# Two key matmuls of the first tile between the opening transposes, and tile 2's copies ahead of the first feature map

## The chip, the cores and the metric

The kernel runs on one core of a Trainium2 chip. The time is the device time of one execution in microseconds (us). A core has a matrix engine (TensorE, "PE" in the profile; its weight loads are "PEld"), a vector engine (VectorE, "DVE"), a scalar engine (ScalarE, "ACT"), GpSimd ("POOL") and SyncE ("SP"), which here only issues transfers. Each engine works through its own queue in order and waits on semaphores of the others. Matmul results land in PSUM, in eight banks of 128 x 512 f32; VectorE and ScalarE read them from there.

## The reference, cut to what matters

```python
qkv = x @ wqkv                       # x: 2048 x 512, 32 heads of 16
phi = lambda t: where(t > 0, t + 1, exp(t)) + 1e-6
pq, pk = phi(q), phi(k)
kv = einsum("bhsd,bhse->bhde", pk, v);  z = einsum("bhsd->bhd", pk)
a  = (pq @ kv) / (pq . z + 1e-6) @ wo          # linear attention
h  = layernorm(x)                              # over the 512 features
b  = (gelu(h^T @ w1 + b1) @ w2 + b2)^T         # MLP over the 2048 tokens
g  = sigmoid((x * gate_w).sum(-1))
out = g * a + (1 - g) * b
```

## The kernel before

The 2048 tokens are 16 tiles of 128 (`NT`), the 512 features 4 blocks of 128 (`ND`). The kernel uses `kv = pk^T v = (x^T pk)^T wv`, so that it needs the keys first and no values: for each tile it makes the keys (`kacc`, four matmuls), their feature map (`pk`), and then adds `x^T pk` to four banks `gacc` (`g_tile`, four matmuls). This key stage takes the first 33 us. After it come the queries (`qacc`) between the first MLP matmuls (`uacc`), the rest of the first MLP layer, and the output loop with `aps` and `yps`.

The schedule is written out by hand (`manual_schedule`): each engine runs its instructions in the order in which the code lists them. Semaphores and the choice of PSUM banks follow from the buffers named; all banks come from one pool of eight (`bank`).

The key matmuls need x with features on the partitions (`xT`). For tiles 3 to 15 a transposing transfer makes it (L135). For tiles 0 to 2 PE transposes: four 128 x 128 matmuls with the identity into a bank `pt`, of which VectorE copies the first half to `xT` (L209) and ScalarE the second (L210). The order around the change is this (L287 to L295):

```python
transpose_tile(0)
transpose_tile(1)
for t in range(2):
    k_part(t, range(2))
transpose_tile(2)
ln_step(0)
for t in range(HEADS):
    k_part(t, range(2 if t < 2 else 0, ND))
    k_phi(t)
```

So PE does the transposes of tiles 0 and 1, the first two of the four key matmuls of tile 0 and of tile 1, the transposes of tile 2, and then the rest. `k_phi` is an exponential on ScalarE (L214), a minimum with one on VectorE (L215) and a combination on VectorE that writes `pk` (L218). `ln_step(u)` is the layernorm statistics of tile u on VectorE (L238, L239), and for each fourth tile a short step towards the inverse deviation (L243 and, on POOL, L244). In the loop that follows, tile t's keys are made, `g_tile` runs four tiles behind (`LAG`) and the statistics three tiles behind (`LN_LAG`); at the end of the stage four `g_tile` calls remain, the last of which needs `pk` of tile 15.

The transfers of the opening: SP's queue brings x tiles 0, 1 and 2 one by one, ScalarE's queue the key weights in two halves. Six matmuls on constants (`wps`) come first on PE.

Of the kernel before, what the change touches and what calls it, by code (L numbers as in the profile page):

```python
# [7 lines left out]
ACT = mybir.ActivationFunctionType  # L8
# [7 lines left out]
def kernel(  # L16
# [13 lines left out]
    nc = tc.nc  # L30
    P = nc.NUM_PARTITIONS
# [9 lines left out]
    ND = D // P  # L41
# [25 lines left out]
    def keep(shape, dtype, name):  # L67
        return persist.tile(shape, dtype, name=name, tag=name)

    def bank(name, dtype=FP32):  # L70
        return ps.tile([P, SC], dtype, name=name, tag="bank")

    xs = keep([P, NT, D], BF16, "xs")
    hs = keep([P, NT, D], BF16, "hs")
    xT = keep([P, ND, S], BF16, "xT")
# [17 lines left out]
    ident = keep([P, P], BF16, "ident")  # L93
# [18 lines left out]
    def mm(o, lhsT, rhs, start, stop, **kw):  # L112
        nc.tensor.matmul(o, lhsT=lhsT, rhs=rhs, start=start, stop=stop, **kw)  # L113
# [20 lines left out]
    def load_xT(t0, n):  # L134
# [14 lines left out]
        out=ident[:], in_=ident[:], compare_op=ALU.not_equal, fill=1.0, base=0,  # L149
# [5 lines left out]
        out=maskQ[:], in_=maskH[:].rearrange("p (a m) -> p m a", m=2), op=ALU.max, axis=AX.X  # L155
# [4 lines left out]
        out=xT[:, :, 3 * P : 3 * P + 2],  # L160
        in_=xs[:, 0, 0 : 2 * ND].rearrange("p (k c) -> p k c", k=ND),
# [10 lines left out]
    for c, (j0, nb) in enumerate(w1_chunks):  # L172
        w = wpool.tile([P, NT, FB * P], BF16, name="w1c", tag="wc")
        w1c.append(w)
        for t0 in range(0, NT, 8) if c < 3 else (0,):
            t1 = t0 + 8 if c < 3 else NT
            nc.sync.dma_start(
                out=w[:, t0:t1, : nb * P], in_=w1_view[:, t0:t1, j0 * P : (j0 + nb) * P]
# [15 lines left out]
    def warm_up(n, cols=SC):  # L194
        for _ in range(n):
            mm(wps[:, :cols], warm[:, 0:P], warm[:, :cols], True, True)
# [2 lines left out]
    nc.scalar.activation(out=act_warm[:], in_=ones_f[:], func=ACT.Exp)  # L199
    warm_up(6)  # L200

    def transpose_tile(t):
        pt = bank("pt")
        for k in range(ND):
            mm(pt[:, k * P : (k + 1) * P], xs[:, t, k * P : (k + 1) * P], ident[:], True, True)
        H = ND // 2
        src = pt[:].rearrange("p (k s) -> p k s", k=ND)
        dst = xT[:, :, t * P : (t + 1) * P]
        nc.vector.tensor_copy(out=dst[:, 0:H], in_=src[:, 0:H])  # L209
        nc.scalar.activation(out=dst[:, H:], in_=src[:, H:], func=ACT.Copy)  # L210

    def phi(dst, acc):
        e = work.tile([P, SC], BF16, name="e", tag="e", bufs=6)
        nc.scalar.activation(out=e[:], in_=acc[:], func=ACT.Exp)  # L214
        nc.vector.tensor_scalar(  # L215
            out=e[:], in0=e[:], scalar1=1.0, scalar2=PHI_EPS, op0=ALU.min, op1=ALU.add
        )
        nc.vector.scalar_tensor_tensor(  # L218
            out=dst, in0=acc[:], scalar=0.0, in1=e[:], op0=ALU.max, op1=ALU.add
        )  # L220
# [3 lines left out]
    def k_part(t, ks):  # L224
        if t not in kaccs:
            kaccs[t] = bank("kacc")
        for k in ks:
            mm(
                kaccs[t][:], xT[:, k, t * P : (t + 1) * P], wk_sb[:, k, :],
                k == 0, k == ND - 1,  # L230
            )

    def k_phi(t):
        phi(pk[:, t, :], kaccs.pop(t))

    def ln_stats(t):
        stats = work.tile([P, nc.vector.BN_STATS_DIM], FP32, name="stats", tag="stats", bufs=2)
        nc.vector.bn_stats(out=stats[:], in_=xs[:, t, :])  # L238
        nc.vector.bn_aggr(out=mv[:, t, :], in_=stats[:])  # L239

    def ln_rstd(g):
        s = slice(g * TPC, (g + 1) * TPC)
        nc.vector.tensor_scalar_add(out=veps[:, s], in0=mv[:, s, 1], scalar1=EPS)  # L243
        nc.gpsimd.tensor_tensor(out=rstd[:, s], in0=veps[:, s], in1=mhalf[:], op=ALU.pow)  # L244
# [36 lines left out]
    def ln_step(u):  # L281
        ln_stats(u)
        if u % TPC == TPC - 1:
            ln_rstd(u // TPC)

    HEADS = 3
    transpose_tile(0)  # L287
    transpose_tile(1)
    for t in range(2):
        k_part(t, range(2))  # L290
    transpose_tile(2)
    ln_step(0)
    for t in range(HEADS):
        k_part(t, range(2 if t < 2 else 0, ND))
        k_phi(t)  # L295
    ln_step(1)
# [159 lines left out]
    for j in range(NB0, NF):  # L456
# [19 lines left out]
        out=gg[:], in0=gth[:], scalar1=0.5, scalar2=0.5, op0=ALU.mult, op1=ALU.add  # L476
    )
    nc.vector.tensor_scalar(
        out=c1[:], in0=gth[:], scalar1=-0.5, scalar2=0.5, op0=ALU.mult, op1=ALU.add
# [3 lines left out]
    for t in range(NT):  # L483
        c, tl = divmod(t, TPC)
        aps = bank("aps")
        for j in range(ND):
# [3 lines left out]
            out=a_sc[:], in_=aps[:], func=ACT.Identity,  # L490
            scale=gg[:, t : t + 1], bias=c2[:, t : t + 1],
        )
        for c0, W in ((0, D - P), (D - P, P)) if t == NT - 1 else ((0, D),):
            cs = slice(c0, c0 + W)
            yps = bank("yps")
            for f in range(NF):
# [6 lines left out]
                out=ot[:, :W], in0=yps[:, :W], scalar=c1[:, t : t + 1], in1=a_sc[:, cs],  # L503
# [35 lines left out]
```

## Time and profile before

| | |
|---|---|
| median of five runs | 164.31 us (164.02 to 164.57) |
| profiled execution, its own time | 164.49 us |
| its span | 162.80 us |
| PE busy | 158.8 us, 98% of the span |
| VectorE busy | 89.9 us, 55% |
| ScalarE busy | 63.1 us, 39% |
| key stage ends (first `uacc` matmul starts) | 33.42 us |

The span runs from the first to the last recorded instruction of the profiled execution; its own time is 1.69 us longer. Starts are counted from the span's start. A matmul of 128 x 512 is shown with a length of 0.38 us, but the next starts before it ends; the distance of starts is what counts. In rows of groups the last part tells how long the engine was idle just before and what ended that.

### The profile page before, as it was taken

To read this page: it belongs to the slowest core of one execution; us is meant where nothing else is said; L and a number is where in the kernel's file an instruction comes from. 1 tells how busy PE (TensorE), PEld (TensorE's weight loads), DVE (VectorE), ACT (ScalarE), POOL (GpSimd) and SP (SyncE) were. 2 spreads that over 40 slices of the span, in tenths; PEclk is the share of its full clock that TensorE was granted. 3 is DMA by queue.
4 is the path that set the end of the run, shared out by engine and by line. 5 is a ranking of instruction groups with operands and counts; after the bars stand their busy time and mean duration, and the time that the engine had idled before them with its cause. 6 is when DMAs were issued, how large, how long until landed. Compare 5 with 4: busy or idle time off the path is not lost.

```text
span 162.8 us, 2191 instructions
## 1 busy us (share of the span) xinstructions
PE 158.8 (98%) x833; PEld 72.6 (45%) x833; DVE 89.9 (55%) x212; ACT 63.1 (39%) x98; POOL 17.4 (11%) x34
## 2 busy tenths in 40 slices
PE   7999999999999999999999999999999999999993
PEld 2444444444444444444444444444444444444452
DVE  1599999967999999509995401256211111111112
ACT  3453284848667473212865113111122222111110
POOL 3000702200010000001515500050000000000000
PEclk9999999999999999999999999999999999999999
DMA  5999999999900006600891699832000001110001
GB/s 168 235 259 215 296 348 322 382 386 385 296 7 0 0 0 214 237 4 0 274 331 61 218 317 316 294 115 83 32 32 32 32 32 38 47 46 33 32 32 32
DMA packets 30569, 25.18 MB, mean 155 GB/s; under 512 B 8480, under 2 KB 29984, under 8 KB 30560
## 3 DMA queue, kind: packets, MB, share of 16 engines
q1 hardware_dynamic: 28288, 21.89, 43.2%
q0 software_dynamic: 1440, 2.38, 5.3%
q10 hardware_dynamic: 832, 0.79, 1.4%
q8 instruction: 6, 0.10, 0.2%
q14 instruction: 3, 0.02, 0.0%
HBM read 21.11 MB, written 2.23 MB: 143 GB/s over the span
## 4 chain that ended last, share of the span: by engine, by line
PE 96%; DMA 2%; SPq 0%; DVE 0%; issue 0%
PE uacc L113 30%; PE yps L113 30%; PE kacc L113 9%; PE gacc L113 9%; PE qacc L113 8%; PE aps L113 8%; DMA xs<-in_A_x_dram 2%; PE denps L113 1%; PE pt L113 1%; PE kvps L113 0%; SPq L129 0%; PE w2ps L113 0%; DVE ot L502 0%; PE pt L332 0%
## 5 line engine op out<-in xcount | busy, mean ns | idle before, releaser
L113 PE MATMUL uacc<-hs,w1c 128*128 128x512 bf16 x224 | 51.3, 379 | 0.0
L113 PE MATMUL yps<-uT,w2c 128*128 128x512 bf16 (+2 forms) x238 | 51.0, 366 | 0.0
L502 DVE SCALAR_TENSOR_TENSOR ot<-yps,c,a_sc 128x512 bf16<-128x512 f32 (+2 forms) x17 | 12.2, 720 | 44.9 <-PE yps L113 44.8
L113 PEld LDWEIGHTS <-w2c 128*128 128x128 bf16 x238 | 22.8, 98 | 25.9
L113 PEld LDWEIGHTS <-w1c 128*128 128x128 bf16 x224 | 21.8, 98 | 26.3 <-issue 0.2
L489 ACT ACTIVATE a_sc<-aps,c,gg 128x512 f32<-128x512 f32 x16 | 12.4, 777 | 46.7 <-PE aps L113 39.9
L326 ACT ACTIVATE uT<-uacc,bcol 128x512 bf16<-128x512 f32 x14 | 9.3, 687 | 21.7 <-PE uacc L113 21.7
L113 PE MATMUL kacc<-wk_sb,xT 128*128 128x512 bf16 x64 | 16.7, 392 | 0.0
L113 PE MATMUL qacc<-xT,wq_sb 128*128 128x512 bf16 x64 | 16.4, 379 | 0.0
L113 PE MATMUL aps<-W2sb,pqT 128*128 128x512 bf16 x64 | 16.4, 379 | 0.0
L113 PE MATMUL gacc<-pk,xs 128*128 128x512 bf16 x64 | 15.9, 379 | 0.0
L254 ACT ACTIVATE hs<-xs,nmr,rstd 128x512 bf16<-128x512 bf16 x16 | 12.8, 806 | 3.1 <-DVE nmr L248 3.1
L214 ACT ACTIVATE e<-qacc 128x512 bf16<-128x512 f32 x16 | 9.6, 597 | 9.2 <-PE qacc L113 9.2
L441 POOL DMA_DIRECT2D rex<-rd_dram x16 | 9.4, 598 | 22.5 <-DVE pqT L443 20.3
L214 ACT ACTIVATE e<-kacc 128x512 bf16<-128x512 f32 x16 | 9.3, 592 | 6.6 <-DVE mv L239 2.3
L113 PEld LDWEIGHTS <-xs 128*128 128x128 bf16 x76 | 7.4, 102 | 9.3 <-DMA xs<-in_A_x_dram 1.2
L218 DVE SCALAR_TENSOR_TENSOR pk<-kacc,e 128x512 bf16<-128x512 f32 x16 | 11.1, 692 | 0.6
L218 DVE SCALAR_TENSOR_TENSOR pqT<-qacc,e 128x512 bf16<-128x512 f32 x16 | 11.1, 692 | 0.6
L238 DVE BATCH_NORM_STATS2 stats<-xs 128x6 f32<-128x512 bf16 x16 | 10.9, 683 | 0.0
L215 DVE TENSOR_SCALAR e<-e 128x512 bf16<-128x512 bf16 x32 | 9.0, 281 | 2.3 <-ACT e L214 2.1
L428 DVE CUSTOM_DVE_ANT_0 junk<-xs,gw_b 128x512 bf16<-128x512 bf16 x16 | 9.8, 685 | 0.0
L279 DVE TENSOR_TENSOR zacc<-zacc,pk 128x512 f32<-128x512 f32 x14 | 9.6, 685 | 0.2
(61 smaller groups left out, 70.6 us busy)
## 6 DMA issues: line engine op xcount, KB each, us to landing
w1c<-in_B_w_dram SPq DMA_DIRECT2D x7, 1024.0 KB, 10.7
w2c<-in_B_w_dram SPq DMA_DIRECT2D x8, 896.0 KB, 6.0
rex<-rd_dram POOLq DMA_DIRECT2D x16, 128.0 KB, 3.8
out_dram<-ot SPq DMA_DIRECT2D x13, 128.0 KB, 1.7
xs<-in_A_x_dram SPq DMA_DIRECT2D x3, 512.0 KB, 4.1
wk_sb<-in_A_wqkv_dram ACTq DMA_DIRECT2D x2, 256.0 KB, 3.4
xs<-in_A_x_dram SPq DMA_DIRECT2D x4, 128.0 KB, 2.7
wq_sb<-in_A_wqkv_dram SPq DMA_DIRECT2D x1, 512.0 KB, 6.2
```

What stands on the lines that cost most here:

```text
L113: nc.tensor.matmul(o, lhsT=lhsT, rhs=rhs, start=start, stop=stop, **kw)
L214: nc.scalar.activation(out=e[:], in_=acc[:], func=ACT.Exp)
L215: nc.vector.tensor_scalar(out=e[:], in0=e[:], scalar1=1.0, scalar2=PHI_EPS, op0=ALU.min, op1=ALU.add)
L218: nc.vector.scalar_tensor_tensor(out=dst, in0=acc[:], scalar=0.0, in1=e[:], op0=ALU.max, op1=ALU.add)
L238: nc.vector.bn_stats(out=stats[:], in_=xs[:, t, :])
L254: nc.scalar.activation(out=hs[:, t, :], in_=xs[:, t, :], func=ACT.Identity, scale=rstd[:, t : t + 1], bias=nmr[:, t : t + 1],)
L279: nc.vector.tensor_tensor(out=zacc[:], in0=first, in1=pk[:, t, :], op=ALU.add)
L326: nc.scalar.activation(out=uT[:, j, :], in_=acc[:], func=ACT.Gelu_apprx_tanh, bias=bcol[:, j : j + 1])
L428: nc.vector.tensor_tensor_reduce(out=junk[:], in0=xs[:, t, :], in1=gw_b[:], scale=1.0, scalar=0.0, op0=ALU.mult, op1=ALU.add, accum_out=gp ...
L441: nc.gpsimd.dma_start(out=rex[:], in_=src.unsqueeze(1).to_broadcast([8, HEAD, SC]))
L489: nc.scalar.activation(out=a_sc[:], in_=aps[:], func=ACT.Identity, scale=gg[:, t : t + 1], bias=c2[:, t : t + 1],)
L502: nc.vector.scalar_tensor_tensor(out=ot[:, :W], in0=yps[:, :W], scalar=c1[:, t : t + 1], in1=a_sc[:, cs], op0=ALU.mult, op1=ALU.add,)
```

## The change

Transposing is done in parts, each with a `pt` bank of its own and one copy, on VectorE or on ScalarE. Tile 0 is split in three: block 0 (VectorE), block 1 (VectorE), blocks 2 and 3 (ScalarE). Tiles 1 and 2 are split in two halves. The first two key matmuls of tile 0 now stand right after tile 0's transposes, ahead of those of tile 1. The rest of tile 0's key matmuls and its feature map stand after tile 2's transposes and ahead of tile 0's statistics (`ln_step(0)`), which stood before all feature maps.

```diff
+    def transpose_part(t, k0, k1, on_act):
+        pt = bank("pt")
+        for k in range(k0, k1):
+            mm(pt[:, k * P : (k + 1) * P], xs[:, t, k * P : (k + 1) * P], ident[:], True, True)
+        src = pt[:, k0 * P : k1 * P].rearrange("p (k s) -> p k s", k=k1 - k0)
+        dst = xT[:, k0:k1, t * P : (t + 1) * P]
+        if on_act:
+            nc.scalar.activation(out=dst, in_=src, func=ACT.Copy)
+        else:
+            nc.vector.tensor_copy(out=dst, in_=src)
+
     def transpose_tile(t):
-        pt = bank("pt")
-        for k in range(ND):
-            mm(pt[:, k * P : (k + 1) * P], xs[:, t, k * P : (k + 1) * P], ident[:], True, True)
-        H = ND // 2
-        src = pt[:].rearrange("p (k s) -> p k s", k=ND)
-        dst = xT[:, :, t * P : (t + 1) * P]
-        nc.vector.tensor_copy(out=dst[:, 0:H], in_=src[:, 0:H])
-        nc.scalar.activation(out=dst[:, H:], in_=src[:, H:], func=ACT.Copy)
+        transpose_part(t, 0, ND // 2, False)
+        transpose_part(t, ND // 2, ND, True)
...
     HEADS = 3
-    transpose_tile(0)
+    transpose_part(0, 0, 1, False)
+    transpose_part(0, 1, 2, False)
+    transpose_part(0, 2, ND, True)
+    k_part(0, range(2))
     transpose_tile(1)
-    for t in range(2):
-        k_part(t, range(2))
+    k_part(1, range(2))
     transpose_tile(2)
+    k_part(0, range(2, ND))
+    k_phi(0)
     ln_step(0)
-    for t in range(HEADS):
+    for t in range(1, HEADS):
         k_part(t, range(2 if t < 2 else 0, ND))
         k_phi(t)
     ln_step(1)
```

## The prediction

> **What bounds the kernel now.** I read the page first, then the chain of waits stage by stage, then the timelines of TensorE (PE) and VectorE (DVE) for the first 34 us. The page's parts 1 and 4:
>
> ```profile
> PE 158.8 (98%) x833; PEld 72.6 (45%) x833; DVE 89.9 (55%) x212; ACT 63.1 (39%) x98; POOL 17.4 (11%) x34
> ...
> PE 96%; DMA 2%; SPq 0%; DVE 0%; issue 0%
> ```
>
> PE is the bound over the whole span, so whatever lengthens PE's queue moves the end one for one: after 36 us no view names a wait of PE longer than 0.4 us. The edit lies in the first 10 us; so the question is which engine ends each wait there. PE's timeline:
>
> ```profile
> 3.36 0.63 PE L113 MATMUL pt<-ident,xs 128*128 128x128 bf16 x4
> 4.25 0.61 PE L113 MATMUL pt<-ident,xs 128*128 128x128 bf16 x4 [0.27 <-DMA xs<-in_A_x_dram]
> 4.66 1.75 PE L113 MATMUL kacc<-wk_sb,xT 128*128 128x512 bf16 x4
> 6.24 0.39 PE L113 MATMUL pt<-ident,xs 128*128 128x128 bf16 x4
> 6.46 3.62 PE L113 MATMUL kacc<-wk_sb,xT 128*128 128x512 bf16 x16
> ```
>
> Columns: start, length, work. Call the transposes of tiles 0, 1, 2 T0, T1, T2 and a tile's key matmuls K0, K1 and so on. From 4.25 PE runs T1, two matmuls each of K0 and K1, T2, the rest, with no hole. The one hole is between T0's last start plus a pitch (3.36 + 4 x 0.107 = 3.79) and tile 1's landing, 4.25. Four key matmuls from 4.66 take 1.58 us up to T2, with starts 0.42 apart; from 6.46 sixteen take 3.46, 0.216 apart. So the array doubles its pace near 6.1.
>
> VectorE's timeline, same columns:
>
> ```profile
> 6.67 0.42 DVE L209 CAST xT<-pt 128x256 bf16<-128x256 f32 x1 [1.34 <-PE pt L113]
> 7.01 0.68 DVE L238 BATCH_NORM_STATS2 stats<-xs 128x6 f32<-128x512 bf16 x1
> 7.72 0.18 DVE L239 BATCH_NORM_AGGREGATE mv<-stats 128x2 f32<-128x6 f32 x1
> 8.03 0.29 DVE L215 TENSOR_SCALAR e<-e 128x512 bf16<-128x512 bf16 x1
> 8.36 0.69 DVE L218 SCALAR_TENSOR_TENSOR pk<-kacc,e 128x512 bf16<-128x512 f32 x1
> ...
> 10.81 0.68 DVE L238 BATCH_NORM_STATS2 stats<-xs 128x6 f32<-128x512 bf16 x1
> 11.53 0.18 DVE L239 BATCH_NORM_AGGREGATE mv<-stats 128x2 f32<-128x6 f32 x1
> 11.63 0.26 DVE L215 TENSOR_SCALAR e<-e 128x512 bf16<-128x512 bf16 x1
> ...
> 31.82 0.69 DVE L218 SCALAR_TENSOR_TENSOR pk<-kacc,e 128x512 bf16<-128x512 f32 x1
> ```
>
> From 8.03 on VectorE shows no idle entry up to the last pk at 31.82: a rigid chain of phi and statistics. Only tile 0's statistics are free: they fill the time in which VectorE would wait for tile 0's exponential. And this chain touches PE once, in the chain of waits:
>
> ```profile
> 29.07 3.45 PE gacc L113 x16
> 32.53 0.03 issue
> 32.56 1.02 PE gacc L113 x4
> ```
>
> The last four gacc matmuls (G15) need pk of tile 15. It ends at 31.82 + 0.69 = 32.51; G15 starts at 32.56. At full pitch it would have started at 32.15 + 0.216 = 32.37, so PE already waits 0.19 us for VectorE. **VectorE's chain, not PE, sets when the key stage ends**, with PE 0.19 behind it.
>
> **What the Trainium skill says.** "TensorE: Matmul & The Clock Gate", What's actually happening: the array runs at half rate until a free-running window of about 3.4 us has been busy. The trace agrees on the two rates (0.427 and 0.216 us a matmul, change near 6.1) and shows no window. "VectorE: DVE Perf Modes", Why PSUM operands drop a tier: an f32 PSUM source goes at one element a cycle; 0.424 us for 256 elements and 0.680 for 512 (gT) give 1.0 ns an element, which agrees. "PSUM — Partial Sum Buffer", PSUM bank collisions raise a hardware error: two engines' accesses to one bank must be ordered, reads too. The waits agree, here one tile's two copies:
>
> ```profile
> ACT xT L210 <- DVE xT L209: 3.0, 3, 1.4
> ```
>
> ScalarE's copy starts only after VectorE's, three times.
>
> **The change part by part.**
>
> *Copies in banks of their own.* T0 gets three banks, T1 and T2 two each. ScalarE's halves no longer follow VectorE's: T0's could start about 0.4 us earlier, T2's too. Tile 0's copy on VectorE becomes two of 128 elements. Not in the trace: 0.424 - 128 x 1.0 = 0.296 us each by the two sizes above (bounds 0.21, a pure half, and 0.42, nothing saved). One instruction more on VectorE, in a stretch where it is idle. No instruction on ACT, POOL or SP moves and no DMA is added, moved or passed.
>
> *K0's first two matmuls before T1.* T0's first part ends at 3.36 + 0.31 = 3.67; its copy runs 3.71 to 4.01 (a wait costs 0.04 in the rows: 3.99 to 4.03), the second to 4.30. With 0.06 to the weight load and 0.10 for it, K0 starts at 4.17 and 4.60. T1 then runs 5.02 to 5.45 in place of 4.25. The hole is hardly filled: 4.17 against 4.25, a gain of 0.08.
>
> *A new stall.* K1 now follows T1 directly and must wait for T1's VectorE copy, which K0's two matmuls used to cover. T1's first half ends at 5.13 + 0.31 = 5.44, the copy at 5.48 + 0.42 = 5.90, K1 starts at 6.06: PE is idle for 6.06 - 5.45 = 0.61. Bounds: 0.5 if load and wait overlap, 0.7 if not. Everything in PE's queue stands behind it: K1, T2, K0's rest. With the pace doubling near 6.12 as before, K1's second is at 6.30 and T2 at 6.52, against 6.24: **PE +0.28**. Tile 2 lands at 1.73 + 4.1 = 5.83 (issue plus its time to landing), so T2 could in no order start before about 5.9.
>
> *T2's copies ahead of the first feature map; statistics of tile 0 after it.* In the program's order VectorE now has T2's copy, phi of tile 0, statistics of tile 0, phi of tile 1. The exponential of tile 0 was held by T2's ACT copy (7.12 to 7.40); now K0's end holds it: its last matmul starts at 6.52 + 4 x 0.056 + 0.216 = 6.96 and ends 0.38 later, 7.34. Exponential 7.39 to 7.99, VectorE's first phi step at 8.02, against 8.03: **-0.01**. The ACT copy (6.95 to 7.33) is off the path; if it took 0.1 us more it would be on it. The statistics leave the free slot and enter the rigid chain: from 10.81 to the next phi step at 11.63 a pair costs **0.82**. The slot they leave, 7.25 to 8.02, stays empty. Below: 0.4 if the first phi could start as soon as tile 2's landing allows (near 7.65); above: 1.1 if the stall is at its upper bound and the clock a little later.
>
> *Banks further on.* By the order of the buffers K5 still waits for pk of tile 1. It ends at 9.97 now and at 10.78 then; K5 starts at 10.78 + 0.28 = 11.06. Cost nothing, with 0.28 of cover left; without it, PE would lose the lack, still inside the slack at G15. K6 to K15 wait for pk four tiles back: K6's slack was 12.51 - 10.90 = 1.6 us, and later ones have more.
>
> *Sum.* pk of tile 15 ends at 32.51 - 0.01 + 0.82 = 33.32; G15 starts 0.81 later. PE's own path comes at 32.37 + 0.28 = 32.65, so its 0.28 lies beside the 0.81 and adds nothing. Everything after is PE's queue, whose feeders shift along with it. Profiled execution: span 162.80 + 0.81, and 1.69 around it, makes 165.30. That run (164.49) lay 0.18 over the median of five, 164.31; so the median forecast is **165.12**, the profiled 165.3.
>
> **Rivals.**
>
> *The clock is released a window later.* Up to 6.12 the array now idles 0.38 + 0.61 us in place of 0.46 in the last 3.4 us. If that no longer counts as busy, half rate lasts some 3.4 us longer (the skill's window, an estimate). T2 then starts at 6.92, K0 ends at 8.40, first phi step 9.08: 1.05 + 0.82 = 1.87, so 166.2. PE's own path is then 2.0 late, about level. For: 70% busy against 87%. Against: release needs no full window even now.
>
> *The chain has hidden slack.* If VectorE took up the 0.82 in its gaps (1.04 us of 24.48 between instructions), only PE's 0.28 less its slack of 0.19 is left: 164.4, no change. Against: those gaps recur after each dependent step.
>
> *Faster: the clock comes early.* With the hole at 3.79 shorter the array may be released near 4.3. K0 then starts 4.17 and 4.39, T1 4.6, K1 5.44, T2 5.9, first phi 7.40: -0.63. With the statistics that is still +0.19, no gain. Only if the first phi step comes before 8.03 - 0.82 = 7.21, or gaps take up as much, does it turn; at the most PE gains 0.34 and the 0.19: 163.8. Against: tile 2's landing.
>
> *The edit does nothing.* The instruction orders of the two programs differ on PE and VectorE as described; this is left with no weight.
>
> **How the numbers follow.** Main case 0.68 (164.7 to 165.5 by the bounds 0.4 and 1.1, rounded), late clock 0.20, hidden slack 0.06, early clock 0.06. The range reaches from the main case's lower end to 166.5, past the late clock's 166.2. 0.2%, or 0.33 us, is about what a measurement can tell from no change: slower 0.88, same 0.06, faster 0.06.
>
> **What would show it.** Right: on PE K0's pair before T1 near 4.2, a hole of 0.6 before K1 near 6.06; on VectorE statistics between the first two phis, first phi step near 8.0 after an idle gap of some 0.8; G15 about 0.8 later, after a wait of about 0.7. Wrong: the last pk not later than 32.7, key matmuls 0.42 apart after 7, or G15 starting without a wait.

## The result, and the profile after

The changed kernel takes 164.98 us (median; 164.47 to 165.38), the kernel before 164.22 (163.91 to 164.81, over more runs than were shown first). The ratio is 1.0037, with a 95% interval of 1.0028 to 1.0046: 0.61 us slower, 0.46 to 0.76 by the interval. The means, 164.89 and 164.28, differ by as much, the medians by 0.76. The profiled execution took 164.80 with a span of 163.1. All these are undisturbed runs, and two of the kernels below, "statistics late only" and "banks and pair later", are compared by such runs alone, since the profiled execution of each was disturbed (169.86 and 211.86 us).

First the page of the changed kernel: engines' busy time, and the chain that ended last by engine.

```profile
PE 158.4 (97%) x833; PEld 72.4 (44%) x833; DVE 89.9 (55%) x213; ACT 63.3 (39%) x98; POOL 17.5 (11%) x34
...
PE 81%; DVE 16%; issue 1%; ACT 0%
```

The busy times have hardly moved. The chain has: before it ran through PE for 96%, now 16% of it is VectorE's. That is the key stage, told in one number. PE's timeline (start, length, work, idle before):

```profile
3.36 0.63 PE L113 MATMUL pt<-ident,xs 128*128 128x128 bf16 x4
4.06 0.95 PE L113 MATMUL kacc<-wk_sb,xT 128*128 128x512 bf16 x2
4.84 0.39 PE L113 MATMUL pt<-ident,xs 128*128 128x128 bf16 x4
5.64 0.61 PE L113 MATMUL kacc<-wk_sb,xT 128*128 128x512 bf16 x2 [0.41 <-DVE xT L211]
6.08 0.39 PE L113 MATMUL pt<-ident,xs 128*128 128x128 bf16 x4
...
28.75 3.62 PE L113 MATMUL gacc<-pk,xs 128*128 128x512 bf16 x16
32.90 1.02 PE L113 MATMUL gacc<-pk,xs 128*128 128x512 bf16 x4 [0.53 <-DVE pk L223]
```

Row 2 is K0's pair, which starts in the old hole. Row 4 has the new stall: the last T1 matmul gives up the array at 5.01 + 0.06 = 5.07, K1 starts at 5.64, so 0.57 us. T2 starts at 6.08, not later than before but 0.16 earlier, since the array had doubled its pace by 4.84 in this execution (T1's four lie 0.06 apart) and did so near 6.1 in the one before. The last row is the wait that costs: G15 could have started at 28.75 + 16 x 0.216 = 32.21 and starts at 32.90, 0.69 later. VectorE's timeline:

```profile
6.39 0.42 DVE L211 CAST xT<-pt 128x256 bf16<-128x256 f32 x1 [0.81 <-PE pt L113]
7.57 0.29 DVE L220 TENSOR_SCALAR e<-e 128x512 bf16<-128x512 bf16 x1 [0.75 <-ACT e L219]
7.89 0.69 DVE L223 SCALAR_TENSOR_TENSOR pk<-kacc,e 128x512 bf16<-128x512 f32 x1
8.50 0.68 DVE L243 BATCH_NORM_STATS2 stats<-xs 128x6 f32<-128x512 bf16 x1
9.22 0.18 DVE L244 BATCH_NORM_AGGREGATE mv<-stats 128x2 f32<-128x6 f32 x1
9.32 0.26 DVE L220 TENSOR_SCALAR e<-e 128x512 bf16<-128x512 bf16 x1
...
32.16 0.69 DVE L223 SCALAR_TENSOR_TENSOR pk<-kacc,e 128x512 bf16<-128x512 f32 x1
```

VectorE idles 0.75 us for tile 0's exponential, the slot that tile 0's statistics used to fill; then the statistics stand between the first two phis. From the first phi step to the start of the last pk it is 32.16 - 7.57 = 24.59, against 31.82 - 8.03 = 23.79 before: 0.80 longer.

### The profile page after: what moved, and what is told of

Its sections match the earlier page's. It is cut to its first block, busy times and chain, and to the rows that moved or that the text cites. A ratio compares the mean times of both kernels' runs of the same rounds, so it can differ in the third digit from the quotient of the medians.

```text
span 163.1 us, 2192 instructions
## 1 busy us (share of the span) xinstructions
PE 158.4 (97%) x833; PEld 72.4 (44%) x833; DVE 89.9 (55%) x213; ACT 63.3 (39%) x98; POOL 17.5 (11%) x34
## 4 chain that ended last, share of the span: by engine, by line
PE 81%; DVE 16%; issue 1%; ACT 0%
PE uacc L113 30%; PE yps L113 30%; PE qacc L113 8%; PE aps L113 8%; DVE pk L223 7%; DVE stats L243 5%; DVE e L220 2%; PE wps L113 2%; DVE mv L244 1%; PE kacc L113 1%; PE gacc L113 1%; PE denps L113 1%; DVE xT L211 0%; ACT e L219 0%; PE kvps L113 0%
```

## The experiments

Each profile gives three numbers: the start of VectorE's first phi step, the start of the last pk, and the start of the first `uacc` matmul, which ends the key stage. The kernel before was run beside each series of experiments, with medians of 164.22 to 164.30; a ratio below is to the runs of its own series.

| kernel | first phi | last pk | between | first uacc | profiled time | time - uacc | median |
|---|---|---|---|---|---|---|---|
| before | 8.03 | 31.82 | 23.79 | 33.42 | 164.49 | 131.07 | 164.22 |
| changed | 7.57 | 32.16 | 24.59 | 33.76 | 164.80 | 131.04 | 164.98 |
| statistics early | 7.24 | 31.04 | 23.80 | 32.74 | 163.79 | 131.05 | 164.18 |
| old PE order | 7.85 | 32.44 | 24.59 | 34.05 | 165.10 | 131.05 | 164.81 |
| banks only | 7.41 | 31.21 | 23.80 | 32.91 | 163.97 | 131.06 | 164.01 |
| one pair later | 7.68 | 31.22 | 23.54 | 33.19 | 164.23 | 131.04 | 164.31 |
| pair twice | 7.54 | 32.92 | 25.38 | 34.53 | 165.59 | 131.06 | 165.49 |
| no warm-up | 8.75 | 33.34 | 24.59 | 34.94 | 166.00 | 131.06 | 166.05 |
| filled hole | 7.97 | 30.85 | 22.88 | 33.47 | 164.53 | 131.06 | 164.12 |
| banks, pair later, again | 7.21 | 30.09 | 22.88 | 32.71 | 163.76 | 131.05 | 164.02 |

The seventh column is the same to 0.03 us in all: whatever differs between these kernels, it differs before the first `uacc` matmul. The fourth is the same to 0.01 us wherever VectorE's queue between the two holds the same work. In the last two rows, where it is shortest, it includes a wait of 0.11 for an exponential of the key loop.

**Statistics early.** The changed kernel with tile 0's statistics back in their slot.

```diff
-    k_part(0, range(2, ND))
-    k_phi(0)
-    ln_step(0)
+    ln_step(0)
+    k_part(0, range(2, ND))
+    k_phi(0)
```

> The changed kernel with one thing undone: the statistics of tile 0 stand ahead of tile 0's feature map again, in the idle slot between tile 2's copy and the first exponential. PE's order is that of the changed kernel. Theory (VectorE's chain decides, and the statistics in it cost 0.82): they cost nothing here, the first phi step comes within 0.15 of where it is in the changed kernel (7.6 to 8.1, by the clock), pk of tile 15 ends 0.7 to 0.8 earlier than in the changed kernel at the same clock, and the time falls by some 0.7, to 164.1 to 164.4, level with before. Rival (PE's stall ahead of tile 1's keys sets the time): nothing is won back, 164.9 to 165.1.

Measured: 164.18, ratio to before 0.999 (0.9979 to 1.0). All of the loss is gone, with K0's pair, the stall and the copies as in the changed kernel. The first phi step came at 7.24, ahead of the 7.6 to 8.1 expected, since T2 came 0.32 earlier than in the changed kernel's profile (5.76); the step follows T2 by 1.48, and by 1.49 there. Two lines of PE's timeline:

```profile
5.32 0.60 PE L113 MATMUL kacc<-wk_sb,xT 128*128 128x512 bf16 x2 [0.41 <-DVE xT L211]
...
28.43 4.48 PE L113 MATMUL gacc<-pk,xs 128*128 128x512 bf16 x20
```

The stall ahead of K1 is still there, with the same 0.41 in brackets. But all twenty gacc matmuls run as one group, without a wait. So the stall is not what cost; the statistics in the chain are.

**Old PE order.** The other half undone; the statistics stay late.

```diff
-    transpose_part(0, 0, 1, False)
-    transpose_part(0, 1, 2, False)
-    transpose_part(0, 2, ND, True)
-    k_part(0, range(2))
-    transpose_tile(1)
-    k_part(1, range(2))
+    transpose_tile(0)
+    transpose_tile(1)
+    for t in range(2):
+        k_part(t, range(2))
```

> The changed kernel with the other thing undone: PE's order is that of before (both opening transposes, then two key matmuls of tile 0 and two of tile 1, then tile 2), with the transposes still in parts with banks of their own and with tile 0's statistics after its feature map. Theory: no hole of 0.6 on PE ahead of tile 1's keys; tile 2's transposes at 6.24 as before at the late clock, first phi step at 7.74 there (0.29 earlier than before, since the exponential no longer waits for two copies in a row), last pk 0.82 - 0.29 = 0.53 later than before: 164.6 to 164.9. Rival (the stall is all of the loss): 164.2, as before.

Measured: 164.81, ratio 1.004 (1.0026 to 1.0053), as slow as the changed kernel. From its chain of waits (start, length, what):

```profile
32.44 0.70 DVE pk L223
33.15 0.04 issue
33.19 1.02 PE gacc L113 x4
```

G15 hangs on the last pk, with no stall ahead of K1 in this kernel.

**Banks only.** The old order of everything, transposes in two parts with a bank each.

```diff
-    k_part(0, range(2, ND))
-    k_phi(0)
-    ln_step(0)
+    ln_step(0)
+    k_part(0, range(2, ND))
+    k_phi(0)
```

(on top of the edit of the old PE order)

> The kernel before with the transposes in two parts with a bank each, nothing moved: PE's order and the place of tile 0's statistics are those of before. Theory: ScalarE's copies start some 0.4 earlier, tile 0's exponential 0.29 earlier, but the statistics of tile 0 then end last (7.9), so the first phi step is at 8.0 in place of 8.03: 164.2, no change. Rival (the further banks cost waits on PE): over 164.5. Rival (the copies in parallel are a gain of their own): 163.9.

Measured: 164.01, ratio 0.9993 (0.998 to 1.0005): no change that the interval shows. The reason given was wrong in one step. VectorE's first phi step came 7.41 - 5.92 = 1.49 after T2's start, against 8.03 - 6.24 = 1.79 before: 0.30 earlier, not 0.03. VectorE's T2 copy now waits for two transposes, not four, and starts 0.32 after T2's start in place of 0.43; the statistics end earlier by as much. The phi step then starts 0.11 after the aggregate (7.30), ahead of its shown end (7.48), while the expectation let it wait for that end. Before, it had to wait for tile 0's exponential (7.40 + 0.60 = 8.00), which trailed two copies in a row; now that ends at 6.78 + 0.60 = 7.38. PE sets the end here: the last pk ends at 31.90, and G15 can't start before 28.60 + 16 x 0.216 = 32.06. So not all of the 0.30 is seen.

**Statistics late only.** The kernel before, with the statistics moved and nothing else.

```diff
     transpose_tile(2)
+    k_part(0, range(2, ND))
+    k_phi(0)
     ln_step(0)
-    for t in range(HEADS):
+    for t in range(1, HEADS):
```

> The kernel before with one thing moved: tile 0's statistics after tile 0's feature map on VectorE (and with it nothing else; PE, banks and copies as before). Theory: the first phi step stays at 8.03, the statistics enter the rigid chain, last pk and the last gacc matmuls 0.82 later: 165.0. Rival (VectorE's gaps take it up): 164.2 to 164.4.

Measured: 164.96, ratio 1.0042 (1.0029 to 1.0055). This one move makes the whole loss.

**One pair later.** The changed kernel, with the statistics of the loop four tiles behind instead of three.

```diff
-    LN_LAG = 3
+    LN_LAG = 4
...
-        if t > LAG:
+        if t > LAG + 1:
             ln_step(t - LN_LAG)
```

> The changed kernel with the statistics in the key loop running four tiles behind in place of three: PE's order, copies and tile 0's statistics stay as changed, but VectorE has one statistics pair and one short step fewer ahead of the pk of tile 15 (they follow it, in a stretch with idle time). Theory (the length of VectorE's chain up to the last pk is what costs): the last pk comes 0.8 to 1.0 earlier, the last gacc matmuls no longer wait, the time falls to that of the kernel with early statistics, 164.0 to 164.4. Rival (it is the place of tile 0's statistics, by what comes right behind them, that costs): 164.9 to 165.1, nothing won.

Measured: 164.31, ratio 0.9989 (0.9978 to 1.0). Tile 0's statistics stand where the change put them, but the chain is 24.59 - 23.54 = 1.05 shorter, by a pair and a short step, and the loss is gone. From its chain of waits:

```profile
29.03 4.32 PE gacc L113 x20
```

So it is the length of the chain that counts, not which statistics are in it.

**Pair twice.** Here `ln_step(0)` is called twice in a row at its new place.

> The changed kernel with tile 0's statistics computed twice in a row at their new place (the second writes the same values). Theory: a second pair of 0.82 on the rigid chain moves the last pk and the end by 0.82 again: 165.7 to 165.9. Rival (VectorE's gaps or PE's slack take up a second one): 165.0 to 165.3.

Measured: 165.49, ratio 1.0062 (1.0043 to 1.0081), a little below the forecast of 165.7. Its profiled execution, with nearly the same opening as the changed kernel's (T2 at 6.05 and 6.08), is 165.59 - 164.80 = 0.79 longer, and its chain 25.38 - 24.59 = 0.79. The last gacc group on PE:

```profile
33.67 1.02 PE L113 MATMUL gacc<-pk,xs 128*128 128x512 bf16 x4 [0.79 <-DVE pk L223]
```

The medians lie only 0.51 apart; which openings the fewer runs of this kernel had isn't known.

**No warm-up.** The changed kernel with `warm_up(0)` in place of `warm_up(6)`.

> The changed kernel without the six matmuls on constants that open PE's queue, to see what a late release of the clock costs. Theory (prediction's rival of the late clock, priced at about 1.1 on top of the statistics): full rate comes only after 8, key matmuls are 0.42 apart up to there, first phi step at 8.6 to 9.1, time 165.7 to 166.9. Rival (the clock follows something other than PE's work, and changes near 4 to 6 all the same): 164.9 to 165.1.

Measured: 166.05, ratio 1.0089 (1.0065 to 1.0112). PE and VectorE:

```profile
6.61 0.63 PE L113 MATMUL pt<-ident,xs 128*128 128x128 bf16 x4
7.04 4.07 PE L113 MATMUL kacc<-wk_sb,xT 128*128 128x512 bf16 x16
```

```profile
8.75 0.29 DVE L220 TENSOR_SCALAR e<-e 128x512 bf16<-128x512 bf16 x1 [1.26 <-ACT e L219]
```

T2's matmuls (row 1) and key matmuls started up to then lie 0.11 and 0.42 apart; of the 3.69 us between the first and last start of row 2, two or three intervals are long, so the pace doubles near 8. The first phi step comes at 8.75, 1.18 later than in the changed kernel's profile, and the chain behind it is 24.59 once more. All four runs (165.48 to 166.24) lie above the changed kernel's 25. So the moment depends on PE's earlier work, and a late doubling costs about what the prediction's rival said, 1.05: in the profiles 1.18, by the medians 1.07, by the ratios 0.85.

**Filled hole, and the same kernel without the filler.** Both are the banks-only kernel with `LN_LAG` at four as above ("banks and pair later"); the first has one matmul on constants more.

```diff
     transpose_tile(0)
+    warm_up(1)
     transpose_tile(1)
```

> The kernel before with transposes in parts with banks of their own, and the statistics in the loop four tiles behind: PE's order and tile 0's statistics as before. Theory: VectorE no longer holds the last gacc matmuls at any clock, PE alone sets the end; against before only its slack of 0.19 at the late clock is won: 163.8 to 164.2. Rival (what moved behind the key stage is then late for the MLP): 164.3 or more.

> The kernel with banks of their own and statistics four tiles behind (old order on PE), plus one matmul on constants between the transposes of tile 0 and tile 1, where PE has its hole of 0.4 to 0.5 ahead of tile 1's landing. Question: does the hole decide when the array doubles its pace? Theory (it does, so that a filled hole brings the change before 5 in most runs, as the changed kernel's order seemed to): the upper half of the times, 164.3 to 164.8, thins out, median 163.8 to 163.9. Rival (the time of the change is a matter of the run, not of the hole): the times lie as without the matmul, in two groups near 163.9 and 164.5, median near 163.95. Filler in the way: above 164.1.

> The same kernel without the extra matmul, on the same chip for comparison: 163.9 to 164.0 in the median; no wait ahead of the last gacc matmuls, last pk at least 0.8 earlier than PE needs it.

Measured: without the filler 163.94 and, in the second series, 164.02; ratios to before 0.9983 (0.9971 to 0.9994) and 0.9978 (0.9963 to 0.9994). With it 164.12, ratio 0.9988 (0.9976 to 1.0). The times keep their spread: 163.64 to 164.51 without, 163.76 to 164.64 with. The profiles contradict the theory outright; first the filled hole, then the open one, PE's timeline:

```profile
3.78 0.63 PE L113 MATMUL wps<-const-bfloat16-1.0 128*128 128x512 bf16 x1
4.39 0.61 PE L113 MATMUL pt<-ident,xs 128*128 128x128 bf16 x4
4.79 1.86 PE L113 MATMUL kacc<-wk_sb,xT 128*128 128x512 bf16 x4
```

```profile
3.37 0.62 PE L113 MATMUL pt<-ident,xs 128*128 128x128 bf16 x4
4.46 0.40 PE L113 MATMUL pt<-ident,xs 128*128 128x128 bf16 x4 [0.47 <-DMA xs<-in_A_x_dram]
4.70 1.18 PE L113 MATMUL kacc<-wk_sb,xT 128*128 128x512 bf16 x4
```

With the hole filled, four key matmuls still lie 0.42 apart and the pace doubles only near 6.5; with it open, T1 already runs at full pace at 4.46. Nor was the filler in the way here: started at 3.78, it takes 0.43 at the slow pace, and T1's first weight load waits for tile 1's landing until later:

```profile
4.39 0.35 PEld L113 LDWEIGHTS <-xs 128*128 128x128 bf16 x4 [0.56 <-DMA xs<-in_A_x_dram]
```

So filling the hole is not enough to bring the doubling forward. The medians, 0.10 apart, don't tell the two kernels apart: each is inside the other's spread.

The kernel without the filler is the best one tried, and below before in both series: 0.06% to 0.29% and 0.06% to 0.37%. In its profile the last pk ends at 30.09 + 0.69 = 30.78, and G15 starts at 32.71 - 0.86 = 31.85, held by PE's own queue.

## Why the prediction was right

*The bound.* "VectorE's chain, not PE, sets when the key stage ends" held: in every profile of the table with a pair more in the chain (changed, old PE order, pair twice, no warm-up), G15 waited for the last pk; where that pair or another was taken out, it didn't.

*Statistics into the chain: +0.82.* Measured 0.80 (24.59 against 23.79), and 0.79 for a second pair. Right, and the main term.

*Copies in parallel.* The prediction put the first phi step 8.02 - 6.52 = 1.50 after T2; 1.49 was measured, against 1.79 before. Right as a length in the traces. In the totals it is not clear of noise: old PE order and statistics late only differ by these copies alone, with ratios of 1.004 and 1.0042.

*The new stall: 0.61.* Measured 0.57. Right as a hole. As a delay of T2, **+0.28**, it was mis-sized: T2 came 0.16 earlier, and the totals show no cost of the new PE order that is clear of noise. By the medians it costs 164.98 - 164.81 = 0.17 with late statistics and 164.18 - 164.01 = 0.17 with early ones; by the ratios to before it gains 0.05 in each pair (1.0037 against 1.004, 0.999 against 0.9993). The intervals of each pair overlap. A part of the reason is in the profiles: the forecast took the doubling at 6.12, as in the one profile at hand. Where it comes by about 5, T2 can be held by tile 2's landing and not by PE's order. T2's first weight load, in banks only (old order) and in pair twice (new order):

```profile
5.91 0.23 PEld L113 LDWEIGHTS <-xs 128*128 128x128 bf16 x4 [0.37 <-DMA xs<-in_A_x_dram]
...
6.05 0.23 PEld L113 LDWEIGHTS <-xs 128*128 128x128 bf16 x4 [0.64 <-DMA xs<-in_A_x_dram]
```

So a part of the stall lies before a landing that PE would wait for anyway. How much of the +0.28 is left when the pace doubles late, no run isolates. The landing also comes earlier than the forecast's "in no order before about 5.9": T2 starts at 5.71 in "banks, pair later, again" and at 5.76 in statistics early.

*The sum.* With the measured 0.80 and -0.30, and -0.05 to 0.17 for the new PE order, it is 0.45 to 0.67; 0.61 was measured, 0.46 to 0.76 by the interval. The forecast's 0.81 lay just above it, by the term of the stall. The forecast median, 165.12, is 0.14 above 164.98, which is in part luck: the profiled execution was forecast at 165.3 and took 164.80, 0.31 above the one before and not 0.81.

*Places.* K0's pair near 4.2: 4.06. First phi near 8.0: it came at 7.57, 0.46 earlier than before and not 0.01, with T2 0.16 earlier and the copies' 0.30. G15's wait of about 0.7: 0.69. This wait doesn't depend on when T2 starts, since T2 shifts both paths: 0.19 + 0.80 - 0.30 = 0.69. G15 later by 0.8: only 0.34, which is 0.80 - 0.46.

*Rivals.* The late clock was in no profile with the warm-up in place, and was priced about rightly when made to happen. Hidden slack in the chain: none, the chain took each pair in full. A gain by an early clock: the changed kernel's own profile had one, and was still slower, as the working said.

## What to carry to other kernels

Before moving work on an engine, ask whether the place it leaves is idle time and whether the place it goes to is a chain without idle entries; the same instructions cost 0 in one and 0.80 us in the other, though the busy sums are equal. An engine at 55% busy can set a stage's end: follow the one consumer that waits for the chain's last link. A hole on the busiest engine (0.57 us here, 97% busy) may cost little, where the stage ends on another engine's chain or a landing would have held the engine anyway.

## What was not expected

The moment when the array doubles its pace is not fixed from execution to execution: with the same six matmuls from 0.84 on, profiles show it between about 4 (pair twice: K0's pair, from 4.06, lies 0.23 apart) and 6.5 (filled hole). By that and the landings, the first phi step differs by 0.64 us between two kernels with one order on PE (7.85 in old PE order, 7.21 in "banks, pair later, again", 1.49 and 1.50 after T2), and a kernel's times spread over up to 1 us. All four profiles of the new PE order with warm-up have the doubling by about 5, of the five with the old order two; whether the order has a part in that stays open. For differences under 1 us the lengths inside one trace (the chain, equal to 0.01 us) told more than two totals.
